# DeltaNet attention and SwiGLU FFN on one core: the engines' order from a build-time planner, or from a stored table

## The chip, the cores and the metric

The kernel runs on one core of one Trainium2 chip. The metric is the device time of one execution in microseconds (us). One more execution is taken by the hardware profiler, which records when each instruction ran on the engines PE (matrix products), DVE and ACT (vector and scalar work), POOL (GpSimd) and SP (it issues most of the transfers).

## The reference: what is computed

Everything is float32. The first half is a delta-rule attention over 4 batches, 8 heads, 768 time steps and heads of 48 elements; its output goes row by row through an RMS norm into a feed-forward block of width 1536 (3072 tokens of 384 elements).

```python
k_n = k / (norm(k) + 1e-06)
for t in range(S):
    y[:, :, t] = einsum('bhd,bhde->bhe', q[:, :, t], state)
    v_old = einsum('bhde,bhd->bhe', state, k_n[:, :, t])
    state = state + beta[:, :, t] * einsum('bhd,bhe->bhde', k_n[:, :, t], v[:, :, t] - v_old)
...
xn = x / sqrt(mean(x * x) + 1e-06) * rms_g
g = xn @ w_gate
out = (g * sigmoid(g) * (xn @ w_val)) @ w_out
```

## The kernel before, in words

**The work.** Time is cut into 12 chunks of 64 steps; a chunk is 256 tokens (4 batches). For each chunk `prep` normalizes and transposes k, forms the products of keys and inverts a triangular matrix per head (in the first two chunks by `invert`, later by a recursion on DVE with detours through DRAM); `qpart` does the query side; `recur` applies the chunk to the state, takes the norm over the 384 elements of each token and transposes the tokens for the feed-forward block (L1250, evicted with the norm's weight by L1259). The tokens of a chunk come in two halves, p = 0 and 1; each has a mean (L1217), a root on POOL (L1224) and a scaling (L1235 on DVE, L1239 on ACT) before L1250. The feed-forward block of chunks 0 and 1 is plain (`ffn_plain`: L1322 up, L1304 down). From chunk 2 on, `ffn` uses a scheme with fewer products: 15 products a half (L1417), whose results are added up in SBUF by DVE (L1427, after a copy by ACT, L1429), Silu on ACT (L1433), the product with the value side on DVE (L1434), and `down` with seven products (L1474) between sums on DVE (L1466, L1483). The weights arrive as 64-bit numbers in 18 loads of 768 KB and are made into float32 by ACT (L504, L505) and DVE (L499, L502). On POOL run the power functions (L613, L632) and, from chunk 4 on, three larger operations of `prep` a chunk (L881, L906, L911).

**What sets the order.** The kernel is not a loop that runs; it is unrolled while it is built. Every piece of work is a step (`Op`) in a plan: its engine, a planned length, the function that emits its instructions, what it reads and writes, and the PSUM banks that it takes and gives back. There are 2702 steps: 610 on PE, 659 on ACT, 929 on DVE, 88 on POOL, 416 transfers on SP. `Plan.run` chooses one order of all steps and calls their functions in it, so each engine gets its instructions in that order, and an engine works through its own in sequence, waiting where an input is late.

Before the change `run` finds the order while the kernel is built. It goes 60 times through `forward`, a list scheduler that keeps a clock for each engine and takes the step that could start first, priorities deciding ties; `backward` turns the result into new priorities, with a little random noise; the order with the earliest planned end is kept.

**Filler.** Until a planned time of 110 us (`UNTIL`) the plan puts padding products (`filler`, L1581, also called by `dense`) where it expects PE to be idle for over 0.8 us; their number is fixed at build time by the planned gap:

```python
while b - a > 0.8 and t < b - 0.1:
    n.append(4 if b - t > 1.0 else 2 if b - t > 0.5 else 1)
    t += 0.215 * n[-1]
```

**Row counts on PE.** A PE step uses the array with 128, 64 or 32 rows (`P.rows`); the plan charges 0.1 us when the next step uses another count.

The functions that the change touches, and what calls them:

Of the kernel before, what the change touches and what calls it, by code (L numbers as in the profile page):

```python
# [4 lines left out]

# [13 lines left out]
C = 64  # L19
W = 32  # L20
DP = 64
STRETCH = {"PE": 1.5, "ACT": 1.5, "DVE": 1.4, "POOL": 1.2, "SP": 1.0}
ENGINES = ("PE", "ACT", "DVE", "POOL", "SP")
OVERLAP = {"PE": 0.0, "ACT": 0.1, "DVE": 0.08, "POOL": 0.06, "SP": 0.0}
ROUNDS = 60
FETCH, AHEAD = 67.0, 160.0
EARLY, FETCH0, AHEAD0 = 130.0, 50.0, 150.0
STICK = 1.0
BEGIN = {"PE": 1.4, "ACT": 0.8, "DVE": 1.0, "POOL": 0.8, "SP": 0.8}
DEEP, SLIP = 7.0, 0.2  # L30
SPARE = 66.0
SHAKE = 0.12


class Op:
# [19 lines left out]
def fillers(a, b):  # L55

    if a == 0.0:
        return [4, 4, 2]
    n, t = [], a
# [3 lines that stand above are left out]
    return n  # L63


class Plan:
# [35 lines left out]
        self.ops.append(op)  # L102
        return op

    def first_priorities(self):
        for op in reversed(self.ops):
            if op.late:
                op.prio = min(
                    (u.prio - (0.0 if u.eng == op.eng and not op.dma else op.lat + u.slack + 0.2) for u in op.users),
                    default=op.prio,  # L110
                ) - STRETCH[op.eng] * op.dur - (3.0 if op.dma else 0.0)
            op.key = op.prio - op.ahead

    def forward(self, banks, until):

        at = dict(BEGIN)
        held = {"DVE": 0.0, "POOL": 0.0}
        cand = {e: [] for e in ENGINES}
        free = list(banks)
        for op in self.ops:  # L120
            op.wait, op.at = len(op.deps), op.ready
            for g in op.acquire:
                g.taken, g.uses = False, g.left
            if not op.wait:
                cand[op.eng].append(op)
        order, server, end_, mode = [], 0.0, 0.0, 0
        lands = []
        backlog = 0.0
        while len(order) < len(self.ops):
            best = None  # L130
            for e in ENGINES:
                first = [(op.urgent, max(op.at, at[e])) for op in cand[e] if op.urgent]
                for op in cand[e]:
                    s = max(op.at, at[e])
                    if op.dma:
                        s = max(s, server - DEEP)
                        if len(lands) >= 8:
                            s = max(s, lands[-8] + op.lat)
                    if any(u > op.urgent and s < t < s + op.dur - SLIP for u, t in first):
                        continue  # L140
                    if op.port:
                        s = max(s, held["POOL" if e == "DVE" else "DVE"])
                    n = sum(not g.taken for g in op.acquire)
                    if n > len(free):
                        continue
                    if n:
                        s = max(s, free[n - 1])
                    key = op.key - op.urgent + (STICK if op.mode is not None and op.mode != mode else 0.0)
                    rate, store = (FETCH, AHEAD) if s > EARLY else (FETCH0, AHEAD0)
                    if op.size and backlog + op.size - rate * op.dur > store:  # L150
                        key += 2.0 * STICK
                    if best is None or (s, key, op.n) < best[0]:
                        best = ((s, key, op.n), op)
            if best is None:
                return None
            (s, _, _), op = best
            cand[op.eng].remove(op)
            for g in op.acquire:
                if not g.taken:
                    g.taken = True  # L160
                    free.pop(0)
            op.start = s
            if op.mode is not None and op.mode != mode:
                s += 0.1
                op.start, mode = s, op.mode
            end = s + op.dur
            if op.eng == "PE":
                if s - at["PE"] > 1.4 and s > until:
                    end += 1.6
                rate, store = (FETCH, AHEAD) if s > EARLY else (FETCH0, AHEAD0)  # L170
                fill = 6.0 if s < until else 0.0
                backlog = max(0.0, backlog - (rate - fill) * (s - at["PE"])) + op.size - rate * op.dur
                late = max(0.0, backlog - store) / rate
                backlog, end = max(0.0, backlog - rate * late), end + late
            at[op.eng] = end - min(OVERLAP[op.eng], op.dur)
            if op.port:
                held[op.eng] = end
            end_ = max(end_, end)
            for g in op.release:
                g.uses -= 1  # L180
                if not g.uses:
                    free.append(end + 0.1)
                    free.sort()
            if op.dma:
                server = max(end + 0.9, server) + op.work
                end = server
                lands.append(end)
            op.end = end
            for u in op.users:
                u.wait -= 1  # L190
                u.at = max(u.at, at[op.eng] if u.eng == op.eng and not op.dma else end + op.hop(u) + u.slack)
                if not u.wait:
                    cand[u.eng].append(u)
            order.append(op)
        self.end = end_
        return order

    def backward(self):

        front = dict.fromkeys(ENGINES, self.end)  # L200
        cand = {e: [] for e in ENGINES}
        for op in self.ops:
            op.wait, op.at = len(op.users), self.end
            if not op.wait:
                cand[op.eng].append(op)
        left = len(self.ops)
        while left:
            best = None
            for e in ENGINES:
                for op in cand[e]:  # L210
                    t = min(op.at, front[e])
                    if best is None or (t, op.start, op.n) > best[0]:
                        best = ((t, op.start, op.n), op)
            (t, _, _), op = best
            cand[op.eng].remove(op)
            op.key = t - op.dur
            front[op.eng] = op.key + min(OVERLAP[op.eng], op.dur)
            for d in op.deps:
                d.wait -= 1
                gap = d.end - d.start - d.dur + (0.0 if d.eng == op.eng and not d.dma else d.hop(op) + op.slack)  # L220
                d.at = min(d.at, op.key - gap)
                if not d.wait:
                    cand[d.eng].append(d)
            left -= 1

    def run(self, free, filler=None, until=0.0):
        self.first_priorities()
        best = None
        self.ends = []
        rng = random.Random(2)  # L230
        for k in range(ROUNDS):
            order = self.forward([t for t, _ in free], until if filler else 0.0)
            if order is None:
                break
            self.ends.append(self.end)
            if best is None or self.end < best[0]:
                best = self.end, [(op, op.start) for op in order]
            self.backward()
            for op in self.ops:
                op.key += SHAKE * (k % 3) * rng.uniform(-1.0, 1.0)  # L240
        self.end = best[0]
        pe = 0.0
        free = list(free)
        for op, s in best[1]:
            op.start = s
            if filler and op.eng == "PE":
                spare = [x for x in free if x[0] == SPARE and s < SPARE or x[0] <= pe]
                if s < until and spare:
                    filler(fillers(pe, s), spare[-1][1])
                pe = s + op.dur  # L250
            for g in op.acquire:
                if g.t is None:
                    g.t = free.pop(0)[1]
            op.fn()
            for g in op.release:
                g.left -= 1
                if not g.left:
                    free.append((s + op.dur + 0.1, g.t))
                    free.sort(key=lambda x: x[0])
# [1357 lines left out]
```

## Time and profile before

| What | Value |
|---|---|
| Median of 3 runs | 680.55 us (680.03 to 680.62) |
| Profiled execution | 681.07 us, its span 679.2 us |
| Mean granted PE clock | 0.997 |
| Busy: PE, DVE, ACT, POOL | 668.9, 526.2, 310.3, 142.4 us |
| PE products in FFN groups L1417 and L1474 | 3240 records |
| Filler products (L1581) | 52 records, 20.3 us |
| Moved by DMA | 55.73 MB, mean 82 GB/s |

The span runs from the first to the last instruction; 1.9 us of the profiled execution lie around it. A group of instructions is one line of the kernel on one engine with its tiles ("out<-in"); the number behind x is how many records it has. One product in float32 leaves two records. In the timeline a row starts with its start and its length in us; a bracket at its end gives how long the engine sat idle before it and what released it, "issue" meaning that nothing in the profile accounts for it. "PEld" is the load of weights into PE, which runs beside the products. SPq is SP's queue issuing a transfer.

### The profile page before, as it was taken

To read this page: it belongs to the slowest core of one execution; us is meant where nothing else is said; L and a number is where in the kernel's file an instruction comes from. 1 tells how busy PE (TensorE), PEld (TensorE's weight loads), DVE (VectorE), ACT (ScalarE), POOL (GpSimd) and SP (SyncE) were. 2 spreads that over 40 slices of the span, in tenths; PEclk is the share of its full clock that TensorE was granted. 3 is DMA by queue.
4 is the path that set the end of the run, shared out by engine and by line. 5 is a ranking of instruction groups with operands and counts; after the bars stand their busy time and mean duration, and the time that the engine had idled before them with its cause. 6 is when DMAs were issued, how large, how long until landed. Compare 5 with 4: busy or idle time off the path is not lost.

```text
span 679.2 us, 23230 instructions
## 1 busy us (share of the span) xinstructions
PE 668.9 (98%) x10038; PEld 616.4 (91%) x10038; DVE 526.2 (77%) x1132; ACT 310.3 (46%) x743; POOL 142.4 (21%) x145
## 2 busy tenths in 40 slices
PE   8989999999999999999999999999999999999997
PEld 5777887777899899999999999999999999999997
DVE  6959898988589799499589589689679658967372
ACT  6477733235345355345345356356245354245240
POOL 2220331004321312312303403502403112000000
PEclk9989999999999999999999999999999999999999
DMA  8949542857613514522723731613521340130101
GB/s 204 325 122 276 161 111 38 153 126 137 112 22 54 107 20 62 100 37 41 128 32 49 129 46 27 121 28 50 99 52 27 68 82 3 29 52 2 24 1 24
DMA packets 216118, 55.73 MB, mean 82 GB/s; under 512 B 205200, under 2 KB 208272, under 8 KB 215696
## 3 DMA queue, kind: packets, MB, share of 16 engines
q1 hardware_dynamic: 214976, 54.05, 40.1%
q8 instruction: 79, 1.29, 0.8%
q10 hardware_dynamic: 1040, 0.20, 0.2%
q14 instruction: 23, 0.19, 0.1%
HBM read 42.94 MB, written 15.20 MB: 86 GB/s over the span
## 4 chain that ended last, share of the span: by engine, by line
PE 86%; DVE 11%; issue 1%; ACT 1%; POOL 1%; DVEq 0%; POOLq 0%; ACTq 0%
PE bank L1417 38%; PE bank L1474 19%; PE bank L1322 7%; PE bank L1304 4%; PE bank L587 3%; PE bank L1040 3%; PE bank L1117 2%; PE bank L1103 2%; PE bank L564 1%; PE bank L1174 1%; DVE tmp L1427 1%; PE bank L1581 1%; PE bank L1250 1%; PE bank L806 1%; PE bank L825 1%
## 5 line engine op out<-in xcount | busy, mean ns | idle before, releaser
L1417 PE MATMUL bank<-xf,w_in 128*128 128x128 f32 x1440 | 180.8, 277 | 0.2
L1417 PEld LDWEIGHTS bank<-xf,w_in 128*128 128x128 f32 x1440 | 170.2, 192 | 2.8 <-issue 1.0
L1427 DVE TENSOR_TENSOR tmp<-tmp,bank 128x512 f32<-128x512 f32 x180 | 121.2, 683 | 65.8 <-PE bank L1417 56.9
L1417 PE MATMUL bank<-xf,more 128*128 128x128 f32 x960 | 125.2, 278 | 0.0
L1417 PEld LDWEIGHTS bank<-xf,more 128*128 128x128 f32 x960 | 115.2, 192 | 2.3 <-DVE tmp L1427 0.4
L1429 ACT COPY tmp<-bank 128x512 f32<-128x512 f32 x120 | 67.9, 587 | 97.7 <-PE bank L1417 62.9
L1433 ACT ACTIVATE tmp<-tmp 128x256 f32<-128x256 f32 x120 | 50.2, 419 | 83.9 <-DVE tmp L1427 83.6
L934 DVE TENSOR_REDUCE acc<-acc 128x30 f32<-128x90 f32 (+4 forms) x150 | 70.9, 473 | 5.2
L632 POOL TENSOR_TENSOR knrm<-ksum,half 128x16 f32<-128x16 f32 x11 | 33.5, 3046 | 169.1 <-DVE ksum L611 169.0
L1474 PE MATMUL bank<-wo_sb,hf 128*128 128x192 f32 x360 | 64.0, 328 | 0.1
L1474 PEld LDWEIGHTS bank<-wo_sb,hf 128*128 128x128 f32 x360 | 58.1, 190 | 0.5
L1434 DVE TENSOR_TENSOR hf<-tmp 128x256 f32<-128x256 f32 x120 | 49.3, 432 | 9.1 <-ACT tmp L1433 8.6
L928 DVE TENSOR_TENSOR acc<-acc,at 128x60 f32<-128x60 f32 (+4 forms) x150 | 51.9, 346 | 3.3 <-POOL at L911 1.5
L954 POOL COPY acc<-acc 128x128 f32<-128x128 f32 x40 | 20.4, 538 | 142.6 <-DVE acc L934 142.1
L1304 PE MATMUL bank<-wo_sb,hf 128*128 128x384 f32 x96 | 34.9, 495 | 0.0
L881 POOL TENSOR_TENSOR at<-at,beta_b 128x1024 f32<-128x1024 f32 x8 | 19.2, 2403 | 73.6 <-DMA at<-dkk 73.6
L1322 PE MATMUL bank<-xp,w_in 128*128 128x256 f32 x144 | 34.0, 383 | 0.0
L1322 PE MATMUL bank<-xf,w_in 128*128 128x256 f32 x144 | 33.2, 383 | 0.0
L1322 PEld LDWEIGHTS bank<-xf,w_in 128*128 128x128 f32 x144 | 26.9, 190 | 5.0 <-issue 0.2
L1322 PEld LDWEIGHTS bank<-xp,w_in 128*128 128x128 f32 x144 | 26.6, 190 | 5.0 <-DVE w_in L502 0.4
L1483 DVE TENSOR_TENSOR tmp<-tmp,bank 128x192 f32<-128x192 f32 x30 | 10.5, 350 | 25.3 <-PE bank L1474 25.3
L1330 ACT ACTIVATE tmp<-bank 128x256 f32<-128x256 f32 x24 | 9.3, 389 | 41.9 <-PE bank L1322 41.9
(202 smaller groups left out, 1033.4 us busy)
## 6 DMA issues: line engine op xcount, KB each, us to landing
at<-dkk SPq DMA_DIRECT2D x20, 256.0 KB, 4.5
vt<-in_v_dram SPq DMA_DIRECT2D x24, 192.0 KB, 4.1
out_dram<-tmp SPq DMA_DIRECT2D x48, 96.0 KB, 2.2
k<-in_k_dram SPq DMA_DIRECT2D x23, 192.0 KB, 5.3
more<-in_moe_w_gate_dram SPq DMA_DIRECT2D x4, 768.0 KB
more<-in_moe_w_out_dram SPq DMA_DIRECT2D x4, 768.0 KB, 4.8
dkk<-kk SPq DMA_DIRECT2D x40, 64.0 KB, 2.0
q<-dq SPq DMA_DIRECT2D x20, 128.0 KB, 3.1
```

Source lines behind the costliest of these rows:

```text
L632: P.add("POOL", 2.95, lambda: nc.gpsimd.tensor_tensor(out=knrm[i2], in0=ksum[i2], in1=half, op=ALU.pow), pn, r=[("ksum", i2), "half"], w=[ ...
L928: nc.vector.tensor_tensor(out=acc[:, 1:3, 0:n, j + 2 : W].rearrange("p a i t -> p i a t"), in0=acc[:, old, 0:n, j : j + 2, None].to_broadc ...
L934: nc.vector.tensor_reduce(out=acc[:, new, 0:n, j + 2 : W], in_=acc[:, lo : lo + 3, 0:n, j + 2 : W].rearrange("p a i t -> p i t a"), axis=A ...
L954: P.add("POOL", 1.2, lambda: spread(xt_, lambda d, t: nc.gpsimd.tensor_copy(out=d, in_=t), True), pi, w=["acc"])
L1304: nc.tensor.matmul(po[p].t[:, 0:DM], hf[:, spot(f), 128 * p : 128 * p + 128], wo_sb[:, spot(f)], start=(f == f0), stop=(f == f1 - 1), skip ...
L1322: nc.tensor.matmul(ps.t[:, TOK * side : TOK * side + TOK], w_in[:, side, h_, 3 * t + i_, n : n + 128], x_[:, 2 * t : 2 * t + 2].rearrange( ...
L1417: nc.tensor.matmul(g.t[:, 128 * z : 128 * z + 128], fac[:, side, 128 * f : 128 * f + 128], xf[:, xs], start=(begin and z == 0), stop=False ...
L1427: P.add("DVE", V(512), lambda t=t, g=g: nc.vector.tensor_tensor(out=t, in0=t, in1=g.t, op=ALU.add), -1, r=[g], w=[tk], last=g)
L1429: P.add("ACT", A(512), lambda t=t, g=g: nc.scalar.copy(t, g.t), -1, r=[g], w=[tk], last=g)
L1433: P.add("ACT", A(256), lambda t=t: nc.scalar.activation(out=t[:, 0:256], in_=t[:, 0:256], func=ACTF.Silu), -1, w=[tk])
L1434: P.add("DVE", V(256), lambda t=t, f0=f0, p=p: nc.vector.tensor_tensor(out=hf[:, spot(f0) : spot(f0) + 2, 128 * p : 128 * p + 128], in0=t[ ...
L1474: nc.tensor.matmul(g.t[:, 0:192], a_[:, f], b_[:, f], start=(begin and f == 0), stop=(f == 5), skip_group_check=True)
```

## The change

`first_priorities`, `forward`, `backward`, the 60 rounds and the constants for them are gone. In their place stands a string, `ORDER`, with two characters for each step, in the order in which all steps are emitted. A character's value is its place in `DIGITS` (91 characters). The method `times`, what is left of `forward`, goes once through that order and sets planned starts, which now serve only to place the filler and to hand out PSUM banks. The steps, their instructions, the buffers and the transfers are the same.

```diff
-STRETCH = {"PE": 1.5, "ACT": 1.5, "DVE": 1.4, "POOL": 1.2, "SP": 1.0}
-ROUNDS = 60
...
+DIGITS = [chr(c) for c in range(35, 127) if chr(c) not in "\\\""]
+BASE = len(DIGITS)
+ORDER = (
+    "#.#+#-##$b#'#3#(#&#4#0#/#>$J$B$H$K$?$I#%$C#*$U#1#)$D#,#2$E$N#C$V$L$X$W$O$Y$M$_#H$@$A$P$`$F$G$]$a$c$Z$d#?$e$T$^$f$S$g"
...
+    "@E@B@;@M@@@C@D@<@F@O@G@N@H@K@J@R@W@L@P@Q@U@T@S@Y@V@X@[@Z@`@a@b@]@^@_"
+)
...
-    def first_priorities(self):
...
-    def forward(self, banks, until):
+    def times(self, order, banks, until):
 
         at = dict(BEGIN)
         held = {"DVE": 0.0, "POOL": 0.0}
-        cand = {e: [] for e in ENGINES}
         free = list(banks)
...
+        for op in order:
+            s = max(op.at, at[op.eng])
...
-    def backward(self):
...
     def run(self, free, filler=None, until=0.0):
-        self.first_priorities()
-        best = None
-        self.ends = []
-        rng = random.Random(2)
-        for k in range(ROUNDS):
...
-        self.end = best[0]
+        number = [DIGITS.index(x) for x in ORDER]
+        order = [self.ops[a * BASE + b] for a, b in zip(number[::2], number[1::2])]
+        self.times(order, [t for t, _ in free], until if filler else 0.0)
         pe = 0.0
         free = list(free)
-        for op, s in best[1]:
-            op.start = s
+        for op in order:
+            s = op.start
             if filler and op.eng == "PE":
```

## The prediction before the run

> **What bounds the kernel now.** The page first.
>
> ```profile
> span 679.2 us, 23230 instructions
> ...
> PE 668.9 (98%) x10038; PEld 616.4 (91%) x10038; DVE 526.2 (77%) x1132; ACT 310.3 (46%) x743; POOL 142.4 (21%) x145
> ...
> q8 instruction: 79, 1.29, 0.8%
> ```
>
> PE is busy in all but 10.3 us. The change neither adds nor removes a matmul of the problem, so what can go is PE time without such a matmul. The groups by line show that some of the 668.9 us is padding:
>
> ```profile
> L1581 PE MATMUL bank<-ident 128*128 128x512 f32 (+2 forms) x52 | 20.3, 535 | 1.4 <-POOL ident masks.py:199 1.4
> ```
>
> These are the plan's filler products; in windows of 5 us all 52 lie before 46 us. So the start, up to the first FFN product (L1322, at 45.5 us), holds about 21 us of padding and idle (start to start of the problem's steps, less their lengths). After it PE hardly waits for anything the profile names (the waits of PE from 48 us on, all of them):
>
> ```profile
> PE bank L1474 <- DVE xp L1466: 0.7, 1, 0.7
> PE bank L1040 <- ACT acc L951: 0.4, 1, 0.4
> ```
>
> The remaining loss there I take from the instruction starts in the timeline, step by step. A product of L1417 that another 128-row product follows starts 0.89 us ahead of it (median of 253); one that a 64- or 32-row matmul follows, 0.99 us (median of 47). Changing the row count thus costs 0.09 us, and the old order changes it 168 times. Taking off each step's usual length and these 0.09 us, real waits stay at 78.7 us (0.30), 123.2 (0.45), 204.6 (0.60), 214.9 (0.37), 221.9 (0.29), 227.2 (0.99) and 351.4 (0.46): 3.5 us together. The last 6 us (last product, one DVE add, the store) follow each other by data and stay.
>
> The start ends like this in the timeline:
>
> ```profile
> 35.06 1.19 PE L1137 MATMUL bank<-vt,mt 64*64 64x48 f32 x34 [1.49 <-issue]
> ...
> 36.23 1.50 SPq L406 DMA_DIRECT2D vt<-in_v_dram  x2
> ...
> 39.84 0.91 ACT L504 ACTIVATE more<-wsum 128x768 f32<-128x768 f32 x1
> 40.02 0.56 POOL L1224 TENSOR_TENSOR rs<-ms,mhalf 128x1 f32<-128x1 f32 x1
> 40.37 1.57 PE L1581 MATMUL bank<-ident 128*128 128x512 f32 x6
> ...
> 41.77 0.49 PE L1250 MATMUL bank<-ident,yn 128*128 128x128 f32 x3
> ...
> 42.30 0.37 ACT L1259 ACTIVATE xp<-bank,g_sb 128x128 f32<-128x128 f32 x1 [1.56 <-PE bank L1250]
> ...
> 43.35 0.41 ACT L1239 ACTIVATE yn<-bank,rs 128x192 f32<-128x192 f32 x1
> ...
> 43.82 0.55 PE L1250 MATMUL bank<-ident,yn 128*128 128x128 f32 x3 [0.69 <-ACT yn L1239]
> ...
> 45.51 2.76 PE L1322 MATMUL bank<-xp,w_in 128*128 128x256 f32 x12
> ```
>
> Two things are to be seen. The scale of token half 1 (rs) is there at 40.58 (40.02 + 0.56), yet ACT uses it (L1239) only at 43.35, because a weight conversion (L504) and two evictions of half 0 (L1259) stand ahead in ACT's order. And PE runs six filler pieces at 40.37 although half 0 was scaled at 39.96 (L1239 for half 0: 39.54 + 0.42).
>
> **The change part by part.** Decoded (place of the first character in DIGITS times 91, plus that of the second, numbering the plan's steps as they are added), the table holds every step once and after its inputs. On its engine another place is held by 444 of PE's 610 steps (1.8 places off on the mean, 20 at most), 541 of ACT's 659, 807 of DVE's 929, 26 of POOL's 88 and 370 of SP's 416. It is a reshuffle nearby, not another schedule. The planner's work at build time costs the chip nothing.
>
> (a) *The end of the start.* In the table ACT runs L1239 of half 1 before the evictions of half 0, with the L504 conversion nine places later; PE takes both L1250 next to each other and the two transposes of k (L564, 1.04 us) after them. DVE takes the scaling of half 0 (L1235) after the mean of half 1 (L1217, 39.68 + 0.16): ready at 39.84 + 0.42 = 40.26, still before PE is free at 40.4. ACT then: the qt copy (L576, 0.59) until 40.55, L1239 of half 1 from 40.58 to 41.0. PE starts L1250 at 40.4 without filler, at 41.9 with all six pieces (their number comes from the new plan's gap, which I have not got). The four ACT evictions begin 0.53 later (41.77 to 42.30) and take 1.4 us at 0.35 each, so L1322 starts at 42.5 to 43.9 in place of 45.5: a gain of 1.6 to 3.0. I take the middle, 2.3.
>
> (b) *Stalls of PE in "issue".* At 28.4 us (0.54) and 33.6 us (1.49) PE waits for nothing that the profile names, while the loads run flat out, and its clock then drops:
>
> ```profile
> 34.00:36.00 2.00, 0.94 (x33) 0.93 (x34) 0.36 (x1) 0.25 (x2) 1.08 (x1) 1.00 1.02 379
> 36.00:38.00 2.00, 2.00 (x53) 1.61 (x53) 1.46 (x4) 1.79 (x8) 0.00 (x1) 0.68 0.33 94
> ```
>
> (Columns: length, busy PE, PEld, DVE, ACT, POOL, granted clock, DMA share, GB/s.) Queue q8 brings 1.29 MB in 79 packets, 64 B for each of PE's 20,076 instructions: it feeds PE, and shares the DMA engines with the loads. The table moves one 768 KB load (a part of w_out, issued at 20.07) behind a load that waits for ACT after 44 us. At 389 GB/s that is 2.0 us less traffic, and the saturated stretch would end near 34 us, where now 35.06 ends the stall. The gain is bounded by 0 and 2.0; an equally long new stall (-2.0) is the other end. I take 1.0, half of the seen stalls, since the traffic shrinks by less than it lasts. [...]
>
> (c) *Row-count changes.* 149 in place of 168: 19 x 0.09 = 1.7 us. PE is the bound around nearly all of them, so it counts in full.
>
> (d) *Waits in the steady part.* The largest comes from a collision (timeline):
>
> ```profile
> 223.69 2.60 POOL L881 TENSOR_TENSOR at<-at,beta_b 128x1024 f32<-128x1024 f32 x1 [3.09 <-DMA at<-dkk]
> ...
> 224.00 3.10 DVE L1466 TENSOR_TENSOR xp<-hf,tmp 128x768 f32<-128x768 f32 x1
> ...
> 227.16 2.22 PE L1474 MATMUL bank<-wo_sb,xp 128*128 128x192 f32 x12 [0.75 <-DVE xp L1466]
> ```
>
> L1466 of this shape takes 0.95 elsewhere; beside POOL's L881 it took 3.10. The table puts this sum and the one before it 6 and 9 places earlier, ahead of L881. The recurrence at 123.2 gets two more products (2.6 us) ahead of it. Against that, PE asks for everything some us earlier, and DVE is at 9.3 to 9.8 of 10 us in most windows from 190 to 270 us. Removing all gives 3.5; new waits of about the same sum give -3.0. I take 1.5, since two of the three longest go by what I can see.
>
> (e) *SP's and POOL's queues.* Beta, v of chunk 1 and k of chunk 2 are issued in another order; each is needed tens of us later, and only (b) shows. Nothing is charged. If that cover were gone, a late v would hold the recurrence of chunk 1 by the 4.1 us of its landing.
>
> **Sum.** 2.3 + 1.0 + 1.7 + 1.5 = 6.5 us. The profiled execution took 681.07 (span 679.2 and 1.9 around it), so 674.6; the median of the runs is 0.5 lower, so 674.0.
>
> **The rivals.**
>
> *More is gained.* No filler before L1250 (3.0), both stalls gone (2.0), every wait gone (3.5), and 1.7: 10.2, so 670.3. For: the stalls end with the load traffic. Against: DVE has no slack in which to be earlier everywhere. 15%.
>
> *DVE takes the start's gain back.* PE starts the FFN earlier, but its weights pass through DVE, which is busy 9.65, 9.59 and 9.83 of 10 us from 50 to 80. Then (a) and (b) turn into a wait for converted weights and 3.2 remain: 677.3. Against: DVE is idle for 4 of 10 us both from 30 to 40 and from 40 to 50, and the table moves conversions up there. 14%.
>
> *Slower: POOL and DVE collide more often.* Each of chunks 4 to 11 has an L881, L906 and L911 on POOL, 5.4 us in all. Three sums of DVE that met them were lengthened by 2.15, 1.09 and 0.73; only the first made PE wait. If the order puts a sum or an L1434 that PE needs at once under POOL in each of the eight chunks, the price is 0.75 (PE's wait) to 2.15 each, middle 1.45: 11.6 less 6.5 makes 685.6. It decides from four or five such collisions on (6.5 / 1.45). Against: the old order met POOL three times in eight. 8%. [...]
>
> *The table doesn't carry over to the chip.* It was made for steps of planned length; if the chip's lengths differ enough, (a) to (c) return as waits: 680.5. Against: most moves are by a place or two, and (c) needs no timing. 5%.
>
> **How the numbers follow.** The forecast has the remaining 58%; its own range, (a) and (d) each off by half, is 671.9 to 676.6. The range for 8 in 10 goes from 670.0 (the larger gain in full) to 678.8 (1.6 from (a), 1.7 from (c), nothing from (b), new waits of 1.5). Faster by over 0.2% (1.4 us, about what a measurement here can tell) takes the forecast, the first two rivals: 87%. Within 0.2%: the last rival, 5%. Slower: 8%.
>
> **What would show it.** Right: the first L1322 at 42.5 to 43.9 us or, with (b), up to 1 us earlier; fewer "issue" us before L1137; L1466 of the 128x768 shape never over 1.2 us; the same 52 fillers or fewer. Wrong: PE waiting for w_in or wo_sb from DVE L502 between 45 and 80 us; DVE rows of 2 us and more beside L881 or L906; PE idle above 10.3 us in spite of fewer fillers.

## The result

| | Median | Runs | Range |
|---|---|---|---|
| kernel before | 680.48 us | 20 | 679.33 to 684.42 |
| changed kernel | 683.27 us | 20 | 679.64 to 688.35 |

The ratio is 1.0041, with a 95% interval of 1.0025 to 1.0058: 0.4% slower, where 1% faster was forecast (674.0, range 670.0 to 678.8). The changed kernel's runs lie far apart: nine are below 683 us, eight at 684 to 688. Its profiled execution, 686.88 us, is one of the long ones. Executions with a lowered clock over their whole span (the profiled one of e1, 842.82 us at 0.753, is one) are left out of all ratios, and no row of them is read.

The functions that the diff removes stood ahead of the rest, so every line of the kernel's body is 35 lower in the changed kernel: L1322 is L1287, L1137 is L1102, L1250 is L1215, L806 is L771, L825 is L790, L502 is L467. The page of the changed kernel, the lines that answer to those shown of before:

```profile
span 685.2 us, 23202 instructions
...
PE 670.5 (98%) x10032; PEld 619.9 (90%) x10032; DVE 522.2 (76%) x1132; ACT 307.7 (45%) x744; POOL 143.1 (21%) x145
...
PEclk9989889999999999999999999999999999999999
```

The work on each engine is the same, except that ACT has one instruction more (744 for 743) and the filler fewer pieces (46 records, 18.0 us). Of the 40 slices of 17.1 us, before had one with a lowered clock (the third, 34 to 51 us); the changed kernel has three, the third, the fifth and the sixth (68 to 103 us).

**Until the first FFN product** 0.54 us were lost, not 3.3 gained. The timeline, from the stall on:

```profile
36.55 1.84 PE L1102 MATMUL bank<-vt,mt 64*64 64x48 f32 x31 [2.04 <-issue]
...
41.32 1.70 PE L1139 MATMUL bank<-u,k 64*64 64x48 f32 x64
...
42.95 1.57 PE L1546 MATMUL bank<-ident 128*128 128x512 f32 x6
...
44.36 0.82 PE L1215 MATMUL bank<-ident,yn 128*128 128x128 f32 x6
...
46.05 1.32 PE L1287 MATMUL bank<-xp,w_in 128*128 128x256 f32 x5
```

(The last row goes on beyond the view.) The last part is what the table was expected to do: both halves pass L1215 in one row, and from the start of L1139 to the first L1287 it takes 4.73 us, where before took 6.85. But L1139 starts 2.66 us later than before. Three things make that up: PE reaches its first L771, the first product of the inversion, 0.89 us later (22.89 against 22.00), the two stalls in "issue" are 0.6 longer (2.04 for 1.49 and 0.59 for 0.54), and 1.17 us go between the stall and L1139, where the clock is at half for 6.8 us in place of 3.4. The windows by 2 us around the end of the stall (36.55) (columns: length, busy PE, PEld, DVE, ACT, POOL, granted clock, DMA share, GB/s):

```profile
34.00:36.00 2.00, 0.51 (x16) 0.39 (x13) 0.64 (x2) 0.00 (x0) 0.33 (x1) 0.95 0.67 247
36.00:38.00 2.00, 1.45 (x29) 1.44 (x28) 0.71 (x2) 1.06 (x2) 0.00 (x0) 0.50 0.07 20
```

The late L771 goes back to ACT. Its rows in the timeline after k has landed:

```profile
5.71 1.28 ACT L573 ACT_TABLE_LOAD   x1 [5.71 <-DMA k<-in_k_dram]
7.01 0.84 ACT L573 ACTIVATE r<-k 128x768 f32<-128x768 f32 x1
7.76 0.57 ACT L541 COPY kt<-bank 128x512 f32<-128x512 f32 x1
...
8.34 1.28 ACT L404 ACT_TABLE_LOAD   x1
```

In the old order the first thing on ACT is a warm-up Silu of two columns (L439, now L404). Its table was loaded at 1.54 us, while nothing else was to do, and served the square of k (L608) too, which ran at 5.66. The table puts the Silu fourth, behind the square and a copy: now the square first loads a table of its own at 5.71, and the Silu another, both on the way to the first inversion.

**From 48 to 100 us** 5.6 us were lost, the largest part. The timeline:

```profile
73.27 1.46 PE L1287 MATMUL bank<-xp,w_in 128*128 128x256 f32 x6
...
74.76 0.96 DVE L467 CUSTOM_DVE_ANT_0 w_in<-kk,tmp 128x1536 uint16<-128x1536 uint16 x1 [1.12 <-PE bank L1287]
...
77.30 0.42 DVE L784 TENSOR_TENSOR kk<-bank,side 128x256 f32<-128x256 f32 x1
...
77.77 2.06 PE L790 MATMUL bank<-kk,x2bd 64*64 64x32 f32 x64 [1.06 <-DVE kk L784]
...
79.75 2.96 PE L1287 MATMUL bank<-xp,w_in 128*128 128x256 f32 x6
...
82.64 3.51 PE L771 MATMUL bank<-mt,m1bd 64*64 64x32 f32 x61
```

DVE waits 1.12 us for a product on PE before it may write converted weights into w_in; four operations queue up behind it, the last of them L784, and PE stands 1.06 us for that. Then the same kinds of rows are 1.7 to 2 times as long: L1287 2.96 for 1.46, L771 3.51 for 2.06 at 74.66. The clock was at 0.5 from 80.2 to 90.4 us. Of the 5.6 us 1.06 are the wait; about 4.5 are left for the slower rows behind it.

**After 100 us** idle time beyond the steps' lengths and row-count changes is 7.4 us, for 6.6 before. The row-count changes are 19 fewer, as counted, and the tail behind the last product is 0.7 longer (4.8 for 4.1). Sum of the parts: 0.5 + 5.6 + 0.8 - 1.6 (18 changes after the start) + 0.7 = 6.0, the difference of the spans.

### The profile page after: what moved, and what is told of

It is laid out like the page before. It is cut to its first block, busy times and chain, and to the rows that moved or that the text cites. A ratio compares the mean times of both kernels' runs of the same rounds, so it can differ in the third digit from the quotient of the medians.

```text
span 685.2 us, 23202 instructions
## 1 busy us (share of the span) xinstructions
PE 670.5 (98%) x10032; PEld 619.9 (90%) x10032; DVE 522.2 (76%) x1132; ACT 307.7 (45%) x744; POOL 143.1 (21%) x145
## 4 chain that ended last, share of the span: by engine, by line
PE 84%; DMA 5%; SPq 4%; DVE 3%; issue 2%; ACT 2%; POOL 1%; ACTq 0%; DVEq 0%
PE bank L1382 35%; PE bank L1439 18%; PE bank L1287 9%; SPq L371 4%; PE bank L1269 4%; PE bank L552 3%; PE bank L1005 3%; PE bank L1082 2%; PE bank L529 2%; PE bank L1068 2%; PE bank L790 1%; PE bank L1139 1%; PE bank L1215 1%; PE bank L771 1%; DMA dkk<-kk 1%
## 5 line engine op out<-in xcount | busy, mean ns | idle before, releaser
L1398 ACT ACTIVATE tmp<-tmp 128x256 f32<-128x256 f32 x120 | 48.4, 417 | 66.5 <-DVE tmp L1392 66.0
L893 DVE TENSOR_TENSOR acc<-acc,at 128x60 f32<-128x60 f32 (+4 forms) x150 | 53.1, 354 | 2.3
L1287 PE MATMUL bank<-xp,w_in 128*128 128x256 f32 x144 | 36.4, 404 | 0.0
L1287 PE MATMUL bank<-xf,w_in 128*128 128x256 f32 x144 | 33.0, 382 | 0.0
L1287 PEld LDWEIGHTS bank<-xp,w_in 128*128 128x128 f32 x144 | 27.8, 199 | 5.4 <-DVE w_in L467 0.6
L1287 PEld LDWEIGHTS bank<-xf,w_in 128*128 128x128 f32 x144 | 27.0, 190 | 5.0 <-DVE acc L899 0.2
L1239 DVE TENSOR_TENSOR xf<-xf 128x256 f32<-128x256 f32 (+1 forms) x70 | 25.7, 400 | 3.2 <-ACT xf L1224 2.8
```

Source lines behind the costliest of these rows:

```text
L893: nc.vector.tensor_tensor(out=acc[:, 1:3, 0:n, j + 2 : W].rearrange("p a i t -> p i a t"), in0=acc[:, old, 0:n, j : j + 2, None].to_broadc ...
L1287: nc.tensor.matmul(ps.t[:, TOK * side : TOK * side + TOK], w_in[:, side, h_, 3 * t + i_, n : n + 128], x_[:, 2 * t : 2 * t + 2].rearrange( ...
L1398: P.add("ACT", A(256), lambda t=t: nc.scalar.activation(out=t[:, 0:256], in_=t[:, 0:256], func=ACTF.Silu), -1, w=[tk])
```

## The experiments

**Theory 1:** three places lose it: the second table load on ACT at the start; a wait at 75 us for data that the waiting instruction doesn't touch, with the low clock that follows; and the stall near 34 us, which the forecast took to be halved. **Theory 2:** the table's order is worse all along, above all because it bundles small matmuls, and mending single places brings little. All times below are medians, each beside the kernel before in the same series of runs; ratios are to that kernel.

| | Change made | us | before | ratio, 95% |
|---|---|---|---|---|
| e1 | table, Silu first | 682.02 | 680.42 | 1.0023 (1.0007 to 1.0039) |
| e2 | table, 338 and 86 exchanged | 680.26 | 680.42 | 1.0002 (0.9989 to 1.0014) |
| e3 | e1 and e2 | 680.14 | 680.42 | 0.9993 (0.9978 to 1.0008) |
| e4 | old order, Silu late | 681.76 | 680.42 | 1.0026 (1.0007 to 1.0044) |
| e5 | table, w_in by part | 679.41 | 680.59 | 0.9980 (0.9968 to 0.9992) |
| e6 | table, filler in the wait | 681.88 | 680.59 | 1.0010 (0.9996 to 1.0024) |
| e7 | old order, late loads | 677.22 | 680.59 | 0.9946 (0.9929 to 0.9963) |
| e8 | old start, table after, w_in by part | 679.16 | 680.59 | 0.9975 (0.9963 to 0.9988) |
| e9 | e5, Silu and identity first | 678.56 | 680.99 | 0.9962 (0.9950 to 0.9973) |
| e10 | e9, late loads | 676.34 | 680.99 | 0.9931 (0.9916 to 0.9947) |
| e11 | e8, late loads | 678.59 | 680.99 | 0.9960 (0.9948 to 0.9973) |
| e12 | old order, identity late | 680.97 | 680.99 | 1.0001 (0.9986 to 1.0015) |
| e13 | e10, small matmuls spread | 675.05 | 680.10 | 0.9915 (0.9900 to 0.9929) |
| e14 | e11, less filler | 676.52 | 680.10 | 0.9945 (0.9925 to 0.9964) |
| e15 | table, late loads alone | 682.09 | 680.10 | 1.0007 (0.9981 to 1.0032) |

### The table load at the start: e1 and e4

```diff
+        order.remove(self.ops[7])
+        order.insert(order.index(self.ops[5]) + 1, self.ops[7])
```

(Step 7 is the Silu, step 5 the constants that it reads.)

> The changed kernel with one step moved: the warm-up Silu (L404 of the changed kernel) stands first on ACT again, as in the old order; every other step stays in the table's order. Theory 1 (the loss is three places: the start's ACT table loads, one false wait at 75 us with the low clock behind it, a longer stall near 35 us): one ACT table load in place of two, the square of k ends about 1.3 us earlier, PE's first L771 at 22.0 to 22.3 instead of 22.9, and the kernel is 0.6 to 1.0 us faster than the changed one, with the stretch of half clock at 80 us still there in about half of the runs: median near 682.5. Theory 2 (the table's order loses in small pieces everywhere, and the start's gain is filled by padding): the first L771 moves, the first L1287 does not move, and the time changes by less than 0.3 us.

682.02 us: 1.3 under the changed kernel by the medians, 1.2 by the ratios (1.0041 to 1.0023), whose intervals overlap. Whether L771 and L1287 moved as expected can't be told, since its profile isn't read. The reverse, in the old order:

```diff
+        late = next(x for x in best[1] if x[0] is self.ops[7])
+        best[1].remove(late)
+        best[1].insert([x[0] for x in best[1]].index(self.ops[129]) + 1, late)
```

> The kernel before with one step moved: the warm-up Silu (L439 of the kernel before) stands behind the square of k and the first transposed k on ACT, as the table has it; the rest is the old order. Theory 1: two ACT table loads, the first L806 at 22.7 to 22.9 instead of 22.0, and the kernel is 0.6 to 1.0 us slower than before, 681.0 to 681.5. Theory 2: the fillers take up the shift, 680.3 to 680.7.

681.76, 1.3 over the kernel before. The two tables are there, at the same places as in the changed kernel, and the first product of L809 (L806 in before) comes at 23.2 us for 22.0:

```profile
5.75 1.28 ACT L611 ACT_TABLE_LOAD   x1 [5.75 <-DMA k<-in_k_dram]
...
8.38 1.28 ACT L442 ACT_TABLE_LOAD   x1
```

In this profile the first FFN product is 0.9 us late too (46.40 us), yet the span is 679.1, as long as before: the wait of PE for L1466 at 227 us, which the prediction showed, is not in this execution. So the size rests on the medians. The second load and the delay behind it come with the step's place; what they cost is about 1.3 us in both runs, a little over the 0.6 to 1.0 expected, and e4's interval leaves room from 0.5 to 3.0 us.

### The wait at 75 us: e2, e3, e5

Step 338 is a product that reads the slices 0, 3 and 6 of one half of w_in; step 86 is a conversion that writes the slices 1, 4 and 7 between them. The plan knows them as separate and gives them no dependency. The table puts 338 directly ahead of 86 (place 277 and 278 of 2702); in the old order 86 came first, by 60 places. First they were exchanged, with no engine's own order changed:

```diff
+        i = order.index(self.ops[338])
+        order[i : i + 2] = order[i + 1], order[i]
```

> The changed kernel with two neighbours exchanged in the order in which the steps are written out: step 338 (PE, L1287) and step 86 (DVE, L467, a weight conversion). They are on different engines, so no engine's own order changes; only the wait of the conversion for the product that was written out just ahead of it goes. Theory 1: L467 does not wait for the product at 74.8 us, PE does not wait 1.06 us for the sum of L784 at 77.8, the half clock from 80 to 90 us is gone, and the median falls by 1.5 to 3.5 us against the changed kernel, to 680 to 681.8, with the runs at 684 to 688 gone or rare. Theory 2: the wait at 77.8 goes but the clock drops at another place, and the median stays within 0.8 us of 683.3.

680.26: 3.0 under the changed kernel, and no run over 682.4. The half clock at 80 us is gone (mean clock 0.996 for 0.987). But the wait has turned round. The waits of PE:

```profile
PE bank L1289 <- DVE w_in L469: 0.9, 2, 0.7
```

(Columns: total, times, longest.) Now the product waits for the conversion. So the two are ordered by whichever is written out first, although they touch different slices. Their address ranges interleave; that this is why they are taken for one is what e5 tests. With both repairs:

> Both edits together: the warm-up Silu first on ACT, and steps 338 and 86 exchanged in the order in which they are written out. Theory 1: the gains add up, 679.0 to 681.0, level with the kernel before or up to 0.2% faster; what is still missing against the forecast lies in the start (the stall near 35 us and the half clock behind it). Theory 2: 682 to 683.5, slower than the kernel before.

680.14, at the upper end; the gain of the Silu hardly shows on top. Its first product of L775 came at 23.6 us, not 22.0: the filler at the start ran at the low clock past the arrival of k (the clock came up at 8.4 us, in before at 6.0; the six pieces from 2.21 us on take 4.64 us, six at 40.37 in before 1.57, and k is there at 5.64), a loss of 0.8 that e9 and e12 look at.

The cause itself is removed by storing the slices by part, 0 to 2 of one part next to each other:

```diff
-                    todo.append((w_in[:, side, half_, i_:9:3], src, [(key, half_, i_)]))
+                    todo.append((w_in[:, side, half_, 3 * i_ : 3 * i_ + 3], src, [(key, half_, i_)]))
...
-                            ps.t[:, TOK * side : TOK * side + TOK], w_in[:, side, h_, 3 * t + i_, n : n + 128],
+                            ps.t[:, TOK * side : TOK * side + TOK], w_in[:, side, h_, 3 * i_ + t, n : n + 128],
```

(and the same renumbering where the later scheme reads w_in).

> The changed kernel in the table's order throughout, but w_in holds its nine slices by part instead of interleaved, so that a conversion (L467) writes three neighbouring slices and no product reads between them. Operations and sizes stay the same. Theory 1 (the wait at 75 us is for data that the conversion does not touch): L467 does not wait for the product of L1287 and the product does not wait for L467 (0.94 us in the exchanged order), PE has no wait over 0.4 us from 70 to 82 us, no half clock there, and the median is 3 to 4.5 us under the changed kernel: 679.0 to 680.3. Theory 2 (the table asks for converted weights too early): the product still waits for L467 near 75 us, and the time is that of the exchange, 680.3, or longer.

679.41. Neither waits for the other; the timeline at the same place:

```profile
71.80 1.24 PE L1287 MATMUL bank<-xp,w_in 128*128 128x256 f32 x5
71.91 0.92 DVE L467 CUSTOM_DVE_ANT_0 w_in<-kk,tmp 128x1536 uint16<-128x1536 uint16 x1
...
72.97 2.06 PE L771 MATMUL bank<-mt,m1bd 64*64 64x32 f32 x64
...
74.87 2.06 PE L790 MATMUL bank<-kk,x2bd 64*64 64x32 f32 x64
```

The conversion runs beside the product, and L790 follows L771 with no gap. 3.9 us of the changed kernel's time hung on this one wait, over half of it through the clock: in e2 PE still waits 0.9 us for the same operation and keeps its full clock there (64 records of L773 behind it take 2.06 us), and 3.0 of the 3.9 are gained already.

### Wait or clock: e6

```diff
+                if op.n == 266:
+                    filler([4, 1], spare[-1][1])
```

> The changed kernel with five filler matmul pieces of 128 columns (about 1.1 us at full clock) on PE ahead of step 266, the one that waits for DVE at 77.8 us. The wait for the data stays; PE is busy in it. Theory 1: the half clock from 80 to 90 us follows from the idle PE, so it goes, and the median falls by 1 to 3 us to 680.5 to 682 although nothing arrives earlier. Rival: the half clock there follows from the mixture of small matmuls and not from the idle 1.06 us; then it stays, and the time is 683 to 684.5.

681.88, inside theory 1's range, but the run doesn't tell the two apart. The only free bank is one that L786 (L784 before the edit) had just been reading, so the filler waited for it as well:

```profile
PE bank L1548 <- DVE kk L786: 1.1, 1, 1.1
```

PE stood idle as long as before, and the profiled execution has a half clock from 76.6 to 80.0 us. The question is left to the clock records of all runs (last section).

### The stall near 34 us: e7

The three weight loads 62, 67 and 72 of the old order, moved on SP behind the loads of v (step 286):

```diff
+        late = [x for x in best[1] if x[0].n in (62, 67, 72)]
+        best[1][:] = [x for x in best[1] if x not in late]
+        i = [x[0].n for x in best[1]].index(286)
+        best[1][i + 1 : i + 1] = late
```

> The kernel before with three weight loads (768 KB each: two parts of w_out, one of w_gate) moved on SP behind the loads of v for chunk 1, so that they are issued after 37 us instead of 20 to 26 us; nothing else moves. If the stalls of PE called issue at 28 and 34 us come from the loads that saturate the DMA engines (theory 1): the traffic at 380 to 400 GB/s ends by about 30 us, the 1.49 us stall is below 0.5, and the kernel is 1.0 to 2.0 us faster than before, 678.5 to 679.5, unless a late weight stops PE between 48 and 60 us. Rival (the stall belongs to the code, not to the traffic): the stall stays at 1.5 us and the time at 680.4.

677.22, 3.4 under before where 1.0 to 2.0 were expected, and all runs within 0.9 us of each other. To the windows of before that the prediction showed, one more of before:

```profile
38.00:40.00 2.00, 2.00 (x84) 2.00 (x84) 0.97 (x3) 1.61 (x7) 1.83 (x3) 0.50 0.89 174
```

And those of e7:

```profile
32.00:34.00 2.00, 2.00 (x72) 2.00 (x74) 1.82 (x5) 0.00 (x0) 0.75 (x2) 1.00 0.00 0
34.00:36.00 2.00, 2.00 (x72) 1.78 (x67) 1.39 (x3) 1.60 (x6) 1.46 (x1) 1.00 0.03 8
36.00:38.00 2.00, 2.00 (x98) 1.74 (x98) 1.39 (x5) 2.00 (x10) 1.29 (x2) 1.00 0.76 145
```

The loads end at about 30.5 us, PE is busy through 34 to 36 where it stood 1.49, and the clock stays at 1.00 where it was 0.68 and 0.50. The short stall (0.54 before) is still there, 0.54 at 29.3 us, while the loads run at 370 to 390 GB/s; only the long one is gone. The first FFN product comes at 42.65 us (45.51 before): the stall and the half clock behind it cost 2.9 us together. In the records of q8, which the prediction takes to feed PE, the packets of this stretch (16,384 bytes each) start at 26.24 and 32.70 us in before, beside loads at 385 to 396 GB/s, and the long stall (33.57 to 35.06) ends 1.3 us after the second has landed; in e7 they start at 26.84 and 30.44, and there is no long stall. A packet held up by the loads fits these times; that PE waited for it is not shown.

### Where the table gains: e8, e9, e10

The old start with the table behind it (`HEAD` holds the first 196 steps of the old order, in the table's code; w_in by part as in e5):

```diff
+        number = [DIGITS.index(x) for x in HEAD]
+        first = [self.ops[a * BASE + b] for a, b in zip(number[::2], number[1::2])]
+        order = first + [op for op in order if op not in first]
```

> The first 196 steps in the old order (the start, to about 46 us), the rest in the table's order, and w_in stored by part as in the run before it. This takes the table's start away and leaves its fewer row-count changes (18 fewer after 46 us, 1.6 us) and its moved sums. Theory 1 (the table gains in the steady part what was forecast for the row counts, and loses only in the start and at 75 us): 0.8 to 1.8 us faster than the kernel before, 678.6 to 679.6. Theory 2 (the table's steady part is no better on the chip): 680.2 or more.

679.16, 1.4 under before: that fits the 18 row-count changes (1.6), though the run doesn't separate them from the moved sums and the small waits. Next the table from the beginning, with the start mended; step 4 makes the identity matrix:

```diff
+        order.remove(self.ops[4])
+        order.insert(0, self.ops[4])
```

> The table's order with three repairs: w_in stored by part, the warm-up Silu first on ACT, and the identity matrix first on POOL (the table makes a mask first, and PE's first filler starts at 2.21 us instead of 1.42). Theory 1 (each of the three costs what it was seen to cost: 3.9, about 1 and 0 to 0.8 us): 0.7 to 1.5 us faster than with the layout alone, 677.9 to 678.9; PE's first L771 at 22.0 to 22.2, the stall called issue near 34 us and one stretch of half clock behind it still there. Theory 2 (what the start loses elsewhere is taken up by the fillers and the loads): as with the layout alone, 679.2 to 679.6.

678.56, inside the range; how much of it is the Silu's and how much the identity matrix's this run doesn't tell. The first product of the inversion is at 22.56, later than expected. The long stall (2.3 us) and one stretch of half clock are still there. Then the loads too:

```diff
+        late = [self.ops[n] for n in (285, 286, 62, 72)]
+        order = [op for op in order if op not in late]
+        i = max(order.index(d) for op in late for d in op.deps if d not in late)
+        order[i + 1 : i + 1] = late
```

> The kernel of the run before this one (table, three repairs) and the loads moved as in the kernel before with late loads: the loads of v for chunk 1 and two weight loads behind them (parts of w_out and w_gate) stand on SP behind the products that read v of chunk 0, about 37 us. Theory 1 (the forecast of 674.0 missed because the stalls near 34 us and the half clock behind them were not removed, and because of the three places): no stall called issue over 0.6 us before 40 us, no half clock, 2.5 to 3.5 us less: 674.5 to 676.5, close to the forecast. Theory 2 (the table's start needs those loads early): PE waits for converted weights between 45 and 65 us, and the time is 677 or more.

676.34, faster than both kernels, if at the upper end: the first FFN product is at 40.57 us and the profiled execution has no half clock left (two of the six runs still have a mean clock of 0.991 and 0.992), but a longer stall of PE stands at 138 us (e13).

### The other three: e11, e12, e14

e11 is e8 with the three loads of e7 moved in its `HEAD` behind step 286:

> The old order up to about 46 us with the three weight loads late (as measured alone: 677.2 us), then the table's order with w_in stored by part (measured with the old start: 1.4 us under the kernel before). Theory 1 (the two gains are in different places and add): 675.4 to 676.2. Theory 2 (with the late loads, the table's order from 46 to 60 us asks for a weight that is not there yet): PE waits for w_in or wo_sb there, 677 to 679.

678.59: a miss. It is 1.4 slower than e7 by the medians, 1.0 by the ratios, with late loads in both. The timeline shows no late weight but six filler pieces in the middle of the FFN:

```profile
53.79 1.57 PE L1556 MATMUL bank<-ident 128*128 128x512 f32 x6
```

The plan took the moved loads to be late and padded for it. With `UNTIL` at 50 in place of 110 they are not written:

> The old start with late loads and the table after it (678.59 us), with the plan's limit for filler pieces lowered from 110 to 50 us, so that the six pieces at 53.8 us (1.4 us in a row of PE, put there because the plan takes the moved loads to be late) are not written. Theory 1 (that run missed by padding that the plan added, not by a late weight): 0.8 to 1.6 us less, 677.0 to 677.8, and PE waits there for no weight. Rival (the next weight is as late as the pieces were long): PE waits for DVE L477 at 54 us in place of the pieces, and the time stays at 678.6.

676.52, 3.6 under before (e11: 2.4), a little better than expected, and PE waits for no weight there. So padding was about 1.2 us of the miss, counting two stalls in "issue" (0.9 and 0.8) that e11's profile has and e14's hasn't. Added up, the two gains would have been 4.8 (3.4 of e7, 1.4 of e8); the other 1.2 us are not explained. In e12 the old order makes the mask first (step 8 moved to the front) and the identity matrix behind it:

> The kernel before with one step of POOL moved: the triangular mask ahead of the identity matrix, as the table has it. PE's fillers start 0.8 us later. Theory 1 (the clock of PE is low until some time after its first work, and the pieces then run past the arrival of k): PE's first product of k (L564) at 5.9 to 6.7 us instead of 5.84, and 0 to 0.8 us slower than before, by where the clock comes up in a run. Theory 2: no change, the pieces are padding.

680.97 and 680.99: no difference. The later start of the filler costs nothing that the median shows.

### Bundled matmuls: e13

In e10 PE stands 2.18 us in the middle of three groups of small matmuls in a row:

```profile
135.96 0.65 PE L955 MATMUL bank<-m1bd,kk 128*32 128x64 f32 x32
136.55 1.15 PE L1013 MATMUL bank<-state,qt 48*64 48x48 f32 x64
137.52 0.66 PE L560 MATMUL bank<-qt,kt 64*64 64x64 f32 x32
140.36 0.69 PE L560 MATMUL bank<-qt,kt 64*64 64x64 f32 x32 [2.18 <-issue]
```

e5 (1.4) and e9 (1.2) have it too. One FFN product, step 520, was put between:

```diff
+        order.remove(self.ops[520])
+        order.insert(order.index(self.ops[479]), self.ops[520])
```

> The table with the three repairs and the late loads (676.34 us), with one FFN product (step 520, L1295 there) moved ahead of the second of three neighbouring groups of 64- and 32-row matmuls (step 479, the scores of chunk 2), in the middle of which PE stood 2.18 us in issue at 138 us. Theory 1 (the table puts 160 small matmuls in a row, fewer row-count changes, and PE uses up its fetched instructions before the next 16 KB packet of q8 comes): the stall there falls below 1.0 us, the median to 674.3 to 675.6. Rival (the packet is held up by the transfers of q and of the output at 136 to 140 us, whatever PE does): a stall of 1.5 us or more stays within 5 us of that place, and the time stays at 676.0 to 676.6.

675.05, the best of all. The stall at L562 (L560 before the edit) is 0.38, and PE waits 0.65 for ACT behind it. So the bundling has a price, about 1 us here by the ratios and by the waits (2.18 less 1.03); the intervals of e10 and e13 overlap. It isn't bundling alone: the changed kernel runs the same groups at 148 us without a stall. That PE had used up its fetched instructions, as theory 1 has it, is not shown.

### The loads alone: e15

> The changed kernel with the loads alone moved (v of chunk 1 and two weight loads behind the products that read v of chunk 0); the Silu, the identity matrix and w_in as the table and the change have them. Theory 1 (stall and half clock in the start cost 2 to 3 us, whatever else is wrong; the false wait at 75 us stays): 1.5 to 3 us less than the changed kernel, 680.3 to 681.8, so slower than the kernel before with the same loads moved by 3 us or more. Rival (the changed kernel's loss is in the loads): 678 or less.

682.09, slightly above the range and 4 to 5 over e7 (4.9 by the medians, 4.2 by the ratios), which has the weight loads late in the old order. The start is mended (first L1291 at 41.38 us), the wait at 73 us isn't: three of its twelve runs, with a mean clock of 0.997 and more, are at 675.7 to 678.0, the other nine at 680 to 686. The rival (678 or less) is out, and late loads don't make up for the false wait. Of the two theories at the head of this section the first holds; the second holds only for the groups at 138 us.

## Why the prediction was wrong, by its own steps

Two terms failed, the stalls (b) and the waits (d), and with them the start ahead of L1139, which the sum put at nothing. In the profiled execution the parts are +2.1 for (a), -0.9 for what lies ahead of it, -1.8 for (b), about +1.6 for (c), -6.4 for (d) and -0.7 for the tail, together -6.0 us, where +6.5 was forecast. In (b) and (d) the wait itself was priced, and the half clock that followed it, 6.8 and 10.2 us long, was not.

**(a) The end of the start: right.** 2.3 us were forecast from L1139 on and 2.1 came (6.85 to 4.73), with all six fillers still there, as the cautious end had it. What failed is the silent assumption that everything ahead of it stays. The list of moved steps (541 of ACT's 659) was counted, and the first of them not looked at: the Silu, fourth in place of first, is worth about 1.3 us by the medians (e1, e4).

**(b) The stalls: wrong in sign.** Forecast +1.0. In the changed kernel they are 0.6 longer and another 1.2 us goes by the clock. That the loads make the long stall was right: with three of them later its 1.49 us are gone (e7); that they do it by holding up q8 was an estimate from the packets' times. But the one load moved was too little: the traffic ended about 1 us earlier, and PE still stood 2.04 us. The size was wrong as well. "Bounded by 0 and 2.0" priced PE's idle time alone; the half clock behind it stood in the same fence and wasn't charged. Stall and clock are worth 2.9 us to the start and 3.4 to the median (e7).

**(c) Row-count changes: right as far as the runs can tell**, 1.6 to 1.7 (e8: 1.4 in all). From a place where PE has done the same steps in both kernels (116.26 us before, 123.08 after) to the end of the last product the changed kernel takes 1.55 us less, with 16 changes fewer (1.4 at 0.09 each); the small waits that went and came on the way are in that as well.

**(d) Waits in the steady part: wrong in sign.** +1.5 was taken; after 100 us it was -0.8. The two named waits went: L1431 at 128x768 (L1466 before) never takes over 1.16 us. But the larger of them, 0.99 us of the 3.5 counted, was no property of the old order. In e4, e7 and e12, the old order with one to three steps moved, this sum takes 1.15 us at most and PE doesn't wait for it; the 3.10 us stand in the one profiled execution of before. To take its going as a gain of the table was to read a single execution as the kernel. Others came in their place, none over 0.6 us that the profile names. The large one, at 75 us, lies before that and within the bound of -3.0 as a wait, not with its clock: 5.6 us in the profiled execution, 3.9 in the median (e5). That two steps without a dependency in the plan could wait for each other wasn't asked: this is the step of the prediction that cost most.

**(e) SP and POOL: nothing, as charged** (e12 0.0; no wait of PE for v or beta).

**The rivals.** The kernel did become slower, but not by the mechanism to which the 8% were given: the only attention or FFN operation of DVE that was stretched by over 0.6 us beside POOL in the changed kernel (an L893, 1.63 us beside L808 at 265 us) stopped nobody. "The table doesn't carry over" came nearest with 680.5 against 683.27, but outside its 0.2% and not for its reason, since (a) and (c) did carry over and the rest was lost at three places that a plan of durations doesn't see: a table load, an order imposed by interleaved addresses, a clock. The forecast's own range doesn't follow either: (a) and (d) each off by half are 1.15 and 0.75 us, 672.1 to 675.9 and not 671.9 to 676.6.

**What would show it.** Three of the signs told rightly against the forecast: first L1287 at 46.05, outside 42.5 to 43.9; more "issue" ahead of L1102; PE idle 14.7 us in place of 10.3. A fourth came in another form: between 45 and 80 us PE waited not for w_in from L467 but for an L784 that stood behind it, and L467 was late because it had waited for PE.

With the three places and the loads mended (e13), the span is 673.4 for 679.2: 5.1 from the start, 1.4 from row counts, less about 0.8 of waits after 48 us. That is nearly the forecast sum, but from the start and the loads, where the forecast had counted on the steady part; that the total comes near it is luck.

## What to carry to other kernels

When an order is changed, look first at what is early and done once (a table load, a constant) and at every pair of neighbours that share a buffer: a plan that knows only durations and its own dependencies sees neither. A stall on PE of about 1 us is charged with the half clock that may follow it (here 10.2 us of it behind 1.06 us at 77 us). A wait seen in one profiled execution is looked for in a second before its removal is counted. And a dense run of small matmuls may stall in "issue" (1.2 to 2.2 us in e5, e9 and e10); one long product among them took most of that away in e13.

## What the runs showed of the hardware

The half clock comes in stretches of 3.41 us (before, 36.72 to 40.13), 6.83 (changed kernel, 35.81 to 42.63) or 10.24 (changed kernel, 80.18 to 90.42), multiples of one length, 3.413 us, on a grid that is fixed within a run: the stretch at 80.18 starts 13 lengths behind the one at 35.81, and the last one, in the tail behind the last product (684.34), 177 lengths behind that; in before the one in the tail (678.42) starts 188 lengths behind the one at 36.72. From run to run the grid lies differently, with its first line at 2.58 us in before and at 1.67 in the changed kernel. Laying that grid over the clock records of the 16 traces other than e1's: a half-clock stretch began 13 times between 7 us and the last products, and 12 times the piece of 3.41 us just before it held 0.98 to 1.90 us of PE idle (1.49 in before, 1.30 and 1.00 in the changed kernel; once 0.31). Of the pieces with at least 0.98 us idle, three (1.03, 1.22 and 1.25) were not followed by one, nor were two right after the clock first came up, at 5 to 6 us (1.24 and 1.31); below 0.95 only that once. That would explain the spread of the changed kernel, though only one of its executions has a trace: its wait at 77 us is 1.06 us long, and where the grid cuts it in two, both parts can lie below 0.95. In e5 an idle time of 1.40 us at 142 us was cut into 0.54 and 0.87, and the clock stayed. Why a stretch lasts one, two or three pieces, and why some idle times are not followed by one, is left open.
